# A prologue in another order: one tap row written and read back to front, w_in in halves on two queues, one staging pool, loads and casts spread over the fill

## The chip, the cores and the metric

The kernel runs on one core of a Trainium2 chip. The metric is the device time of one execution in microseconds (us); the runs before the change are three, and their median counts. Engines are named as the profile names them: PE is TensorE (PEld its weight loads), DVE is VectorE, ACT is ScalarE, POOL is GpSimd, SP is SyncE, which here only issues DMAs. ACT can issue DMAs too, on a queue of its own.

## The reference: what is computed

Two steps on x of 8 sequences, 4096 positions, 192 channels. First a causal convolution along the sequence with 7 taps, one set of taps for each of 8 heads of 24 channels, the taps being a softmax of `weight`. Then a two-layer network on every position:

```python
w = softmax(weight)                      # 8 heads x 7 taps
out[b, s, h] = sum_k w[h, k] * x_pad[b, s + k, h]
h = out.reshape(32768, 192) @ w_in       # 192 x 2048
g = h * cos(h)
return g @ w_out                         # 2048 x 192, float32
```

## The kernel before

**Layout.** The 8 sequences are 4 pairs (HB = 4): sequence b and sequence b + 4 go through together, each in one half (a lane) of 64 partitions. x is loaded in units: a unit is 4 blocks of 128 positions (112 new, 16 of overlap) of both sequences, two DMAs of 384 KB (`load_unit`, L83), staged as float32 (`xw`) and cast to bf16 (`xb`).

**The convolution** is a matrix product: for each head a 128x128 band matrix holds the 7 taps on diagonals, so a block of 128 positions times the band gives the 112 new ones. A work item is a pair of parts (a part is one unit and one of three channel groups of 64), 1024 columns in a PSUM tile `h` of two banks. The pool of `h` has three such tiles, for convolutions and for the network alike. In the normal form the product is split into two passes: `conv_first` (L249) uses the upper 64 partitions for one part and the lower 64 for the other, `conv_second` (L263) the other way round and adds. Between the passes a one-element memset on POOL (`changeover`, L199, tile `mark`) waits for the first pass and releases the second. `conv_out` (L266) copies the sum to bf16 (`ct`) on ACT or DVE and a DMA on SP transposes it to `cT`, channels by positions.

**The network** runs in steps of 128 of the 2048 hidden columns and 512 positions of both sequences: U (`up`, L293) makes `h` from `w1` (bf16 w_in) and `cT`; S (`sin`, L302) makes the cosine on ACT; M (`mult`, L307) makes g on DVE; 16 steps make a tile of positions. d (`down`, L314) multiplies g by `w2` (bf16 w_out) into two accumulators; x and y store them.

**The order** is written out by hand as a string of letters that `emit` (L349) reads; C, c and e are the two passes and the way out of a convolution. Each engine runs its instructions in that order. The prologue (L78 to L171, L375 to L386) loads and prepares everything; a fill follows (17 steps U, three convolutions, no d), and then one string is repeated until the end:

```python
emit("USM" * 2 + ("CUScMe" + "USM" * 3) * 3 + "USM" * 2 + "U")
while count["y"] < 2 * NI:
    emit("dddSMdUdMSdUdMSdUMdSUdSMdUdSMCdcdeMUdSdUyxUMS")
```

**The prologue's order.** On SP: wq (the taps' weights, sent to all 128 partitions, L79), six loads of units 0 and 1, eight pieces of w_in (L158: four chunks of 512 columns, each sent to both halves of the partitions), units 2 and 3, three transposes, four pieces of w_out (L168). On DVE and ACT the softmax is made on 128 partitions alike, seven products put the taps into `taps` (L132), and ACT writes all 128 rows to DRAM (L138) and reads them back shifted by one element a row, which makes the band (L139). POOL casts, in this order: halves of units 0 and 1, all of w_in, then the first marker, two parts of x, all of w_out, then the next marker. `prepare` (L238) casts the next pair and loads ahead after every second pass.

Of the kernel before, what the change touches and what calls it, by code (L numbers as in the profile page):

```python
# [16 lines left out]
def kernel(  # L17
# [29 lines left out]
    T = 512  # L47
# [16 lines left out]
    stage = ctx.enter_context(tc.tile_pool(name="stage", bufs=2))  # L64
    xw_pool = ctx.enter_context(tc.tile_pool(name="xw", bufs=3))
# [9 lines left out]
    ctx.enter_context(tc.manual_schedule())  # L75


    wq = consts.tile([128, H, K], FP32)  # L78
    nc.sync.dma_start(out=wq, in_=dram(weight, 0, [[0, 128], [1, H * K]]))  # L79

    xbs = {}

    def load_unit(b, u):  # L83

        xw = xw_pool.tile([128, 2, NB, D], FP32, name="xw")
        xb = xb_pool.tile([128, 2, NB, D], BF16, name="xb")
        if u == NU:
            rows = TAIL + 16
            nc.gpsimd.memset(xw[L:128, :, 0, :], 0.0)
            for s in range(2):  # L90
                base = ((s * HB + b) * S + UT * u - 16) * D
                nc.sync.dma_start(out=xw[0:rows, s, 0, :], in_=dram(x, base, [[D, rows], [1, D]]))
        elif u == 0:
            nc.gpsimd.memset(xw[0:16, :, 0, :], 0.0)
            for s in range(2):
                base = (s * HB + b) * S * D
                nc.sync.dma_start(out=xw[16:128, s, :, :], in_=dram(x, base, [[D, W], [W * D, NB], [1, D]]))
# [16 lines left out]


    ROW = H * 128 + 128
    taps = consts.tile([128, ROW], BF16)
    nc.gpsimd.memset(taps, 0.0)
    wmax = consts.tile([128, H], FP32)
    nc.vector.tensor_reduce(out=wmax, in_=wq, axis=AX.X, op=ALU.max)  # L120
    nc.vector.tensor_tensor(out=wq, in0=wq, in1=wmax.unsqueeze(2).to_broadcast([128, H, K]), op=ALU.subtract)  # L121
    wex = consts.tile([128, H, K], FP32)
    nc.scalar.activation(out=wex, in_=wq, func=AF.Exp)  # L123
    wsum = consts.tile([128, H], FP32)
    nc.vector.tensor_reduce(out=wsum, in_=wex, axis=AX.X, op=ALU.add)
    nc.vector.tensor_scalar(out=wsum, in0=wsum, scalar1=1e-9, scalar2=None, op0=ALU.add)
    winv = consts.tile([128, H], FP32)
    nc.vector.reciprocal(winv, wsum)
    tap = taps[:, 0:H * 128].rearrange("p (h j) -> p h j", h=H)
    for k in range(K):  # L130
        j = 127 - 10 - k
        nc.vector.tensor_tensor(out=tap[:, :, j:j + 1], in0=wex[:, :, k:k + 1], in1=winv.unsqueeze(2), op=ALU.mult)  # L132

    rows_d = d_pool.tile([128, ROW], BF16)
    band = consts.tile([128, H, 128], BF16)
    nc.scalar.dma_start(out=rows_d, in_=taps)  # L138
    nc.scalar.dma_start(out=band, in_=dram(rows_d, rows_d.offset + 127, [[ROW - 1, 128], [1, H * 128]]))  # L139
    warm = consts.tile([128, 1], FP32)  # L140
    nc.scalar.activation(out=warm, in_=winv[:, 0:1], func=AF.Sin, bias=0.0, scale=0.0)  # L141

    for u in range(2):
        load_unit(0, u)
        xw, xb = xbs[(0, u)]
        nc.gpsimd.tensor_copy(out=xb[:, 0, :, :], in_=xw[:, 0, :, :])
        nc.vector.tensor_copy(out=xb[:, 1, :, :], in_=xw[:, 1, :, :])  # L147


    w1 = consts.tile([128, NCH, Dff], BF16)  # L150
    w2 = consts.tile([128, NF, D], BF16)
    CW = Dff // 4

    def load_w1(c):
        cols = slice(c * CW, (c + 1) * CW)
        st = stage.tile([128, NCH, CW], FP32, name="st")
        for s in range(2):
            nc.sync.dma_start(out=st[s * L:(s + 1) * L], in_=dram(moe_w_in, c * CW, [[Dff, L], [L * Dff, NCH], [1, CW]]))  # L158
        if c == 0:
            nc.vector.tensor_copy(out=w1[:, 0:2, cols], in_=st[:, 0:2, :])  # L160
            nc.gpsimd.tensor_copy(out=w1[:, 2:, cols], in_=st[:, 2:, :])
        else:
            nc.gpsimd.tensor_copy(out=w1[:, :, cols], in_=st)  # L163

    def load_w2(c):
        n = NF // 4
        st = stage.tile([128, n, D], FP32, name="so")
        nc.sync.dma_start(out=st, in_=moe_w_out[c * CW:(c + 1) * CW, :].rearrange("(n p) d -> p n d", p=128))  # L168
        nc.gpsimd.tensor_copy(out=w2[:, c * n:(c + 1) * n, :], in_=st)  # L169

    load_w1(0)  # L171


    lane = (slice(0, L), slice(L, 128))
# [24 lines left out]
    def changeover(end):  # L199

        ins = nc.gpsimd.memset(mark, 0.0)  # L201
        order(ins, end)
        return ins
# [23 lines left out]
    pairs = []  # L227
    for b in range(HB):
        for u in range(1, NU, 2):
            pairs += [((b, u - 1, c), (b, u, c)) for c in range(NCH)]  # L230
# [7 lines left out]
    def prepare():  # L238

        c = state["cast"]  # L240
        if c < NC:
            for p in pairs[c]:
                cast_part(*p)
            state["cast"] += 1
        while state["loaded"] <= need[min(c + 2, NC - 1)]:
            load_unit(*units[state["loaded"]])
            state["loaded"] += 1

# [14 lines left out]
    def conv_second(mms, after):  # L263
        lanes(*mms, after=after)

    def conv_out(both, ps, copy=nc.scalar.copy):  # L266
# [14 lines left out]
        if u0 == u - 1 and u < NU:  # L281
            nc.sync.dma_start_transpose(out=dst(ch, u0, u + 1), in_=ct[0:W].rearrange("p k t -> p (k t)"))  # L282
        else:
            nc.sync.dma_start_transpose(out=dst(c0, u0, u0 + 1), in_=ct[0:W, 0, :])
# [64 lines left out]
    def emit(ops):  # L349
# [3 lines left out]
        for op in ops:  # L353
# [4 lines left out]
            elif op == "c":  # L358
                if "open" in state:
                    conv_second(state["open"][2], state.pop("mark"))  # L360
                    prepare()
            elif op == "e":
                if "open" in state:
                    conv_out(*state.pop("open")[:2])
# [7 lines left out]
                else:  # L372
                    {"U": up, "S": sin, "M": mult, "d": down}[op](n)

    for c in range(1, 4):  # L375
        load_w1(c)
    for u in (2, 3):
        load_unit(0, u)
    opened = [conv_first() for _ in range(3)]
    relay = changeover(opened[2][3])  # L380
    prepare()
# [39 lines left out]
```

## Time and profile before

| | before |
|---|---|
| runs | 759.79, 759.84, 759.93 us; median 759.84 |
| profiled execution | 760.31 us, span of its instructions 758.5 |
| PE busy | 709.8 us, 94% |
| DVE, ACT, POOL busy | 645.2, 589.8, 85.7 us |
| DMA | 73.49 MB, mean 97 GB/s |

All times in the profile count from the first instruction of the span. The timeline gives for each row its start, its length, the engine (a q behind it is the engine's issue of a DMA), the line, the operation with the tile it writes and those it reads, the shapes and the count; in brackets is the idle time of the engine before it, and what ended that. The windows view gives busy times by stretch. The DMA issues give size and median time from issue to landing.

### The profile page before, as it was taken

How to read it: one execution, taken by the hardware profiler on the slowest of the kernel's cores; microseconds unless marked ns; L12 is line 12 of the kernel's file. 1: busy time of each engine (PE TensorE's matmuls, PEld its weight loads, DVE VectorE, ACT ScalarE, POOL GpSimd, SP SyncE). 2: the span in 40 equal slices, each digit the busy share in tenths (PEclk: the TensorE clock that was granted, in tenths of full speed). 3: DMA queues.
4: the chain of work that ended last, by engine and by line, in shares of the span. 5: the costliest groups of instructions: out<-in, count | busy, mean ns of one | idle time of the engine just before them, and what ended most of it. 6: DMA issues, size and time to landing. Idle time of an engine off the chain costs nothing.

```text
span 758.5 us, 26895 instructions
## 1 busy us (share of the span) xinstructions
PE 709.8 (94%) x12064; PEld 518.3 (68%) x12064; DVE 645.2 (85%) x592; ACT 589.8 (78%) x639; POOL 85.7 (11%) x247
## 2 busy tenths in 40 slices
PE   0358999999999999999999999999999999999997
PEld 0125777777777777777777777777777777777776
DVE  1058999989898998899898999989899999999992
ACT  1157888888888888888888888888888878788781
POOL 2221011101101110110111011101101100000000
PEclk9999999999999999999999999999999999999999
DMA  8952543426163644242715435426173221111112
GB/s 209 227 148 61 109 110 82 110 73 143 59 168 87 125 90 106 77 116 71 185 37 149 114 78 105 110 76 143 50 179 75 44 56 44 45 43 34 33 44 64
DMA packets 128099, 73.49 MB, mean 97 GB/s; under 512 B 54000, under 2 KB 126192, under 8 KB 127984
## 3 DMA queue, kind: packets, MB, share of 16 engines
q1 hardware_dynamic: 127696, 71.22, 38.4%
q8 instruction: 94, 1.54, 0.9%
q10 hardware_dynamic: 288, 0.56, 0.3%
q14 instruction: 21, 0.17, 0.1%
HBM read 33.71 MB, written 25.46 MB: 78 GB/s over the span
## 4 chain that ended last, share of the span: by engine, by line
PE 91%; DMA 4%; DVE 2%; ACT 1%; issue 1%; POOL 1%; SPq 1%; POOLq 0%; ACTq 0%
PE h L191 46%; PE acc L191 44%; DMA st<-in_moe_w_in_dram 2%; DVE g L309 2%; DMA so<-in_moe_w_out_dram 1%; DMA xw<-in_x_dram 1%; ACT cos L304 1%; SPq L282 0%; POOL w L163 0%; POOL w L169 0%; ACT ct L274 0%; SPq L158 0%; ACT osb L343 0%; DVE osb L343 0%; SPq L98 0%
## 5 line engine op out<-in xcount | busy, mean ns | idle before, releaser
L309 DVE TENSOR_TENSOR g<-h,cos 128x1024 bf16<-128x1024 f32 x512 | 609.9, 1221 | 45.7 <-ACT cos L304 33.8
L304 ACT ACTIVATE cos<-h 128x1024 bf16<-128x1024 f32 x512 | 515.0, 1025 | 113.2 <-PE h L191 95.3
L191 PE MATMUL acc<-w,g 64*128 64x192 bf16 x8192 | 428.1, 243 | 1.3 <-ACT osb L343 0.8
L191 PEld LDWEIGHTS <-g 64*128 64x128 bf16 x8192 | 353.2, 94 | 101.8 <-issue 1.2
L191 PE MATMUL h<-cT,w 64*128 64x512 bf16 x3072 | 410.8, 379 | 10.3 <-DMA cT<-ct 5.0
L191 PEld LDWEIGHTS <-w 64*128 64x128 bf16 x3072 | 148.7, 94 | 89.3 <-issue 16.8
L201 POOL MEMSET mark<- 1x1 f32 x118 | 10.5, 89 | 632.5 <-PE acc L191 453.6
L191 PE MATMUL h<-xb,band 64*128 64x192 bf16 (+4 forms) x800 | 45.3, 230 | 32.9 <-DMA band<-rows_d 19.4
L274 ACT CAST ct<-h 112x1024 bf16<-112x1024 f32 x51 | 51.6, 1013 | 25.8 <-PE h L191 20.6
L343 DVE COPY osb<-acc 128x384 f32<-128x384 f32 x64 | 35.7, 558 | 38.4 <-PE acc L191 38.3
L113 POOL CAST xb<-xw 128x512 bf16<-128x512 f32 x102 | 60.1, 618 | 3.5 <-DMA xw<-in_x_dram 2.6
L191 PEld LDWEIGHTS <-band 64*128 64x128 bf16 x800 | 28.1, 97 | 44.8 <-POOL mark L201 22.4
L343 ACT COPY osb<-acc 128x384 f32<-128x384 f32 x64 | 30.4, 475 | 11.1 <-PE acc L191 11.1
L274 DVE CAST ct<-h 112x1024 bf16<-112x1024 f32 x1 | 1.2, 1224 | 13.7 <-PE h L191 13.7
L141 ACT ACT_TABLE_LOAD x1 | 1.3, 1283 | 10.0 <-DVE w L160 10.0
L163 POOL CAST w<-st 128x1536 bf16<-128x1536 f32 x3 | 4.4, 1469 | 7.6 <-DMA st<-in_moe_w_in_dram 7.6
L169 POOL CAST w<-so 128x768 bf16<-128x768 f32 x4 | 3.3, 824 | 10.5 <-DMA so<-in_moe_w_out_dram 10.5
L120 DVE TENSOR_REDUCE wmax<-wq 128x8 f32<-128x56 f32 x1 | 0.2, 210 | 4.8 <-DMA wq<-in_weight_dram 4.8
L147 DVE CAST xb<-xw 128x768 bf16<-128x768 f32 x2 | 1.1, 560 | 3.6 <-DMA xw<-in_x_dram 3.6
L160 DVE CAST w<-st 128x1024 bf16<-128x1024 f32 x1 | 0.7, 694 | 3.0 <-DMA st<-in_moe_w_in_dram 3.0
L271 ACT CAST ct<-h 112x512 bf16<-112x512 f32 x4 | 2.3, 587 | 0.9 <-PE h L191 0.9
L123 ACT ACTIVATE wex<-wq 128x56 f32<-128x56 f32 x1 | 0.3, 251 | 3.3 <-DVE wq L121 3.3
(18 smaller groups left out, 14.6 us busy)
## 6 DMA issues: line engine op xcount, KB each, us to landing
xw<-in_x_dram SPq DMA_DIRECT2D x64, 384.0 KB, 4.6
out_dram<-osb SPq DMA_DIRECT2D x64, 384.0 KB, 3.4
st<-in_moe_w_in_dram SPq DMA_DIRECT2D x8, 384.0 KB, 7.2
xw<-in_x_dram SPq DMA_DIRECT2D x8, 336.0 KB, 4.7
so<-in_moe_w_out_dram SPq DMA_DIRECT2D x4, 384.0 KB, 4.5
cT<-ct SPq DMA_TRANSPOSE x64, 3.4
xw<-in_x_dram SPq DMA_DIRECT2D x8, 60.0 KB, 1.9
xw<-in_x_dram SPq DMA_DIRECT2D x8, 36.0 KB, 3.9
```

The lines of the kernel that those rows point to most:

```text
L113: nc.gpsimd.tensor_copy(out=xb[:, :, :, ch], in_=xw[:, :, :, ch])
L141: nc.scalar.activation(out=warm, in_=winv[:, 0:1], func=AF.Sin, bias=0.0, scale=0.0)
L147: nc.vector.tensor_copy(out=xb[:, 1, :, :], in_=xw[:, 1, :, :])
L163: nc.gpsimd.tensor_copy(out=w1[:, :, cols], in_=st)
L169: nc.gpsimd.tensor_copy(out=w2[:, c * n:(c + 1) * n, :], in_=st)
L191: ins = nc.tensor.matmul(out=o, lhsT=w, rhs=r, start=start, stop=stop, skip_group_check=True)
L201: ins = nc.gpsimd.memset(mark, 0.0)
L271: nc.scalar.copy(ct[0:W, 0, :], ps[0:W, 0, :])
L274: copy(out=ct[0:W], in_=ps[0:W])
L304: nc.scalar.activation(out=cos, in_=hs[n], func=AF.Sin, bias=math.pi / 2.0, scale=1.0)
L309: nc.vector.tensor_tensor(out=g, in0=hs.pop(n), in1=cs.pop(n), op=ALU.mult)
L343: copy(out=osbs[k][:, 2 * bank:2 * bank + 2, :].rearrange("p a d -> p (a d)"), in_=acc[bank][:, 0:2 * D])
```

## The change

- The softmax is made on one partition. wq is loaded by ACT's queue instead of SP's; one product makes all taps. One row of 2.3 KB is written to DRAM by SP, behind the loads of x, and read back by SP to 128 partitions, each starting one element later (`turned`). The band is then `turned` with its columns read backwards, one half copied by DVE, the other by ACT.
- The casts of units 0 and 1 go to POOL and ACT instead of POOL and DVE.
- Of w_in each chunk's upper half goes on SP's queue and the lower on ACT's. It is cast in thirds (`cast_w1`), w_out is loaded in two pieces instead of four and cast in quarters of them (`cast_w2`). w_in and w_out use the same staging pool as x, now six buffers instead of three; the separate pool `stage` is gone.
- The first three pairs are convolved with all 128 partitions at once, without passes and marker. For units 2 and 3 the pairs are put together so that the first needs unit 2 alone.
- Loads and casts that stood ahead of the fill, or in `prepare`, are jobs in a generator; a letter k in the fill's string takes the next. `prepare` is split into `cast_pair` and `load_ahead`, called together by the letter p in the steady string.

The core of the diff (renamed and moved code that the text above tells is left out):

```diff
-    nc.sync.dma_start(out=wq, in_=dram(weight, 0, [[0, 128], [1, H * K]]))
+    nc.scalar.dma_start(out=wq, in_=dram(weight, 0, [[0, 1], [1, H * K]]))
...
-    for k in range(K):
-        j = 127 - 10 - k
-        nc.vector.tensor_tensor(out=tap[:, :, j:j + 1], in0=wex[:, :, k:k + 1], in1=winv.unsqueeze(2), op=ALU.mult)
+    nc.vector.tensor_tensor(out=tap[:, :, 9:9 + K], in0=wex, in1=winv.unsqueeze(2).to_broadcast([1, H, K]), op=ALU.mult)
...
-    nc.scalar.dma_start(out=rows_d, in_=taps)
-    nc.scalar.dma_start(out=band, in_=dram(rows_d, rows_d.offset + 127, [[ROW - 1, 128], [1, H * 128]]))
+    nc.sync.dma_start(out=row_d, in_=taps)
+    nc.sync.dma_start(out=turned, in_=dram(row_d, row_d.offset, [[1, 128], [1, H * 128]]))
+    for (u, s), copy in (((0, 0), nc.gpsimd.tensor_copy), ((0, 1), nc.scalar.copy),
+                         ((1, 0), nc.gpsimd.tensor_copy), ((1, 1), nc.scalar.copy)):
+        xw, xb = xbs[(0, u)]
+        copy(out=xb[:, s, :, :], in_=xw[:, s, :, :])
...
+    nc.vector.tensor_copy(out=band[:, 0:H // 2, :], in_=flip(turned[:, 0:H // 2, :]))
+    nc.scalar.copy(band[:, H // 2:H, :], flip(turned[:, H // 2:H, :]))
...
+        st = staged[1, c] = staging([NCH, CW])
+        for s, queue in enumerate((nc.sync, nc.scalar)):
+            queue.dma_start(out=st[s * L:(s + 1) * L], in_=dram(moe_w_in, c * CW, [[Dff, L], [L * Dff, NCH], [1, CW]]))
...
+            if (b, u) == (0, 3):
+                single = [(b, v, c) for v in (u - 1, u) for c in range(NCH)]
+                pairs += list(zip(single[::2], single[1::2]))
...
-    opened = [conv_first() for _ in range(3)]
-    relay = changeover(opened[2][3])
-    prepare()
-    for k, o in enumerate(opened):
-        conv_second(o[2], relay)
-        conv_out(*o[:2], nc.vector.tensor_copy if k == 1 else nc.scalar.copy)
-    for c in range(4):
-        load_w2(c)
-
-    emit("USM" * 2 + ("CUScMe" + "USM" * 3) * 3 + "USM" * 2 + "U")
+    for c in range(3):
+        ps = h_pool.tile([128, 2, T], FP32, name="h")
+        for k, p in enumerate(pairs[c]):
+            for o, h, r, _ in part_mms(p, ps[:, k, :]):
+                nc.tensor.matmul(out=o, lhsT=band[:, h, :], rhs=r, start=True, stop=True)
+        conv_out(pairs[c], ps, nc.vector.tensor_copy if c == 1 else nc.scalar.copy)
+    state["conv"] = 3
+    cast_w1(0, 0, nc.vector.tensor_copy)
+    cast_w1(0, 1)
+    cast_w1(0, 2, nc.vector.tensor_copy)
...
+    def later():
+        yield from (lambda q=q: cast_w1(1, q) for q in range(NCH))
+        yield lambda: load_unit(0, 2)
+        yield lambda: load_w1(2)
+        yield lambda: [load_unit(0, 3), load_w1(3), load_w2(0), load_w2(1)]
+        yield cast_pair
+        yield from (lambda q=q: cast_w1(2, q) for q in range(NCH))
+        yield cast_pair
+        yield load_ahead
+        yield from (lambda q=q: cast_w1(3, q) for q in range(NCH))
+        yield cast_pair
+        yield from (lambda c=c, q=q: cast_w2(c, q) for c in range(2) for q in range(4))
+        yield cast_pair
...
+    fill("kkkkUkSkMUSMUSMkUSMUSMCUScMekkkUSMkkUSMUSMCUScMekkkUSMkUSMkkkkUSMCUScMekkkkUSMUSMkU")
     while count["y"] < 2 * NI:
-        emit("dddSMdUdMSdUdMSdUMdSUdSMdUdSMCdcdeMUdSdUyxUMS")
+        emit("dddSMdUdMSdUdMSdUMdSUdSMdUdSMCdcpdeMUdSdUyxUMS")
```

How the order changes on POOL and on ACT, from the casts of units 0 and 1 into the fill. POOL before the change (st and so are the staged w_in and w_out, w_134 and w_135 their bf16 copies, mark the markers):

```order
L146 CAST xb<-xw 128x768 x2
L161 CAST w_134<-st 128x512
L163 CAST w_134<-st 128x3x512 x3
L201 MEMSET mark 1x1
L113 CAST xb<-xw 128x8x64 x2
L169 CAST w_135<-so 128x768 x4
L201 MEMSET mark 1x1
```

POOL after the change (everything is staged in xw; w_128 is w_in, w_129 w_out):

```order
L152 CAST xb<-xw 128x768 x2
L175 CAST w_128<-xw 128x512 x4
L119 CAST xb<-xw 128x8x64 x2
L218 MEMSET mark 1x1
L175 CAST w_128<-xw 128x512 x3
L119 CAST xb<-xw 128x8x64 x2
L218 MEMSET mark 1x1
L175 CAST w_128<-xw 128x512 x3
L119 CAST xb<-xw 128x8x64 x2
L185 CAST w_129<-xw 128x384 x4
L218 MEMSET mark 1x1
```

The first marker had all four chunks of w_in ahead of it and the second all of w_out; now the first one that is left has a third of chunk 0 and chunk 1 ahead of it, the second chunk 2, and the third chunk 3 and the first half of w_out.

ACT before the change, from the exponential of the softmax to the first cosines (rows_d is the DRAM copy of the tap rows):

```order
L123 ACTIVATE wex<-wq 128x56
L138 DMA rows_d<-taps 128x1152
L139 DMA band<-rows_d 128x1024
L141 ACT_TABLE_LOAD
L141 ACTIVATE warm<-winv 128x1
L274 CAST ct<-h 112x1024 x2
L304 ACTIVATE cos<-h 128x1024 x3
```

ACT after the change (the DMAs of in_moe_w_in are the lower halves of w_in's chunks):

```order
L131 ACTIVATE wex<-wq 1x56
L133 ACT_TABLE_LOAD
L133 ACTIVATE warm<-wex 1x1
L152 CAST xb<-xw 128x768 x2
L160 COPY band<-turned 128x512
L172 DMA xw<-in_moe_w_in_dram 64x3x512 x2
L297 CAST ct<-h 112x1024 x2
L172 DMA xw<-in_moe_w_in_dram 64x3x512
L327 ACTIVATE cos<-h 128x1024
L172 DMA xw<-in_moe_w_in_dram 64x3x512
```

The two DMAs of the taps went to SP; two casts of x and half the flip came, and four DMAs of w_in, two of them between the flip and the first ct.

More of the change, by code (lines that the diff above doesn't have):

```diff
@@ L116 @@
     ROW = H * 128 + 128
-    taps = consts.tile([128, ROW], BF16)
+    taps = consts.tile([1, ROW], BF16)
     nc.gpsimd.memset(taps, 0.0)
-    wmax = consts.tile([128, H], FP32)
+    for u in range(2):
+        load_unit(0, u)
+    wmax = consts.tile([1, H], FP32)
     nc.vector.tensor_reduce(out=wmax, in_=wq, axis=AX.X, op=ALU.max)
-    nc.vector.tensor_tensor(out=wq, in0=wq, in1=wmax.unsqueeze(2).to_broadcast([128, H, K]), op=ALU.subtract)
-    wex = consts.tile([128, H, K], FP32)
+    nc.vector.tensor_tensor(out=wq, in0=wq, in1=wmax.unsqueeze(2).to_broadcast([1, H, K]), op=ALU.subtract)
@@ L140 @@
[L140 to L144, printed above, removed]
-        xw, xb = xbs[(0, u)]
-        nc.gpsimd.tensor_copy(out=xb[:, 0, :, :], in_=xw[:, 0, :, :])
-        nc.vector.tensor_copy(out=xb[:, 1, :, :], in_=xw[:, 1, :, :])
+    tap = taps[:, 128:ROW].rearrange("p (h j) -> p h j", h=H)
+    nc.vector.tensor_tensor(out=tap[:, :, 9:9 + K], in0=wex, in1=winv.unsqueeze(2).to_broadcast([1, H, K]), op=ALU.mult)
@@ L171 @@
     load_w1(0)
+    load_w1(1)
     lane = (slice(0, L), slice(L, 128))
@@ L236, with cast_pair, load_ahead @@
     state = {"conv": 0, "loaded": 4, "cast": 3}
[L238 to L242, printed above, removed]
+    def cast_pair():
+        if state["cast"] < NC:
+            for p in pairs[state["cast"]]:
                 cast_part(*p)
             state["cast"] += 1
-        while state["loaded"] <= need[min(c + 2, NC - 1)]:
+    def load_ahead():
+        while state["loaded"] <= need[min(state["cast"] + 1, NC - 1)]:
             load_unit(*units[state["loaded"]])
@@ L360, in emit @@
                     conv_second(state["open"][2], state.pop("mark"))
-                    prepare()
+            elif op == "p":
+                cast_pair()
+                load_ahead()
             elif op == "e":
```

68 lines of the change are left out of this document (39 added, 29 removed).

## The prediction

> **What bounds the kernel now.** I read the page first, then the windows by stage, then the timeline and the waits of the first 66 us.
>
> The page's slices (a slice is 19 us) show TensorE nearly idle in the first two, half used in the third, and full after that:
>
> ```profile
> span 758.5 us, 26895 instructions
> PE   0358999999999999999999999999999999999997
> ```
>
> The windows view, cut at the first w_out product (65.54) and at the start of the fill (36.44). Columns: stretch, its length, busy time of PE, PEld, DVE, ACT, POOL, the granted clock, the DMA share, GB/s.
>
> ```profile
> 11.50:14.50 3.00, 0.00 (x0) 0.00 (x0) 0.30 (x1) 0.00 (x0) 0.00 (x0) 1.00 1.06 291
> 18.50:20.50 2.00, 1.08 (x18) 1.04 (x20) 0.00 (x0) 0.00 (x0) 1.47 (x1) 1.00 1.04 229
> 26.00:30.00 4.00, 1.46 (x20) 1.04 (x20) 0.82 (x1) 1.25 (x2) 2.11 (x3) 1.00 1.11 326
> 31.00:35.50 4.50, 1.22 (x4) 0.24 (x5) 0.00 (x0) 0.00 (x0) 0.61 (x1) 1.00 0.89 161
> 36.44:65.54 29.10, 17.48 (x136) 7.42 (x134) 17.47 (x15) 18.66 (x19) 6.92 (x13) 1.00 0.54 146
> 65.54:754.40 688.86, 687.51 (x11884) 508.21 (x11880) 622.43 (x561) 565.71 (x614) 68.61 (x219) 1.00 0.36 89
> ```
>
> From 65.54 to 754.40 TensorE works 687.51 of 688.86 us. The steady loop's text is unchanged apart from a `prepare` split into `cast_pair` and `load_ahead` called together, so I move this block as a whole: **the new time is the old one minus what the first w_out product gains on 65.54.** Everything is decided ahead of it, and there the timeline shows these steps:
>
> ```profile
> 0.75 0.41 SPq L79 DMA_DIRECT2D wq<-in_weight_dram  x1
> 1.21 0.42 SPq L97 DMA_DIRECT2D xw<-in_x_dram  x1
> 4.85 0.21 DVE L120 TENSOR_REDUCE wmax<-wq 128x8 f32<-128x56 f32 x1 [4.85 <-DMA wq<-in_weight_dram]
> 6.39 0.66 DVE L132 TENSOR_TENSOR taps<-wex,winv 128x8 bf16<-128x8 f32 x7
> 9.12 0.83 POOL L146 CAST xb<-xw 128x768 bf16<-128x768 f32 x1 [1.41 <-DMA xw<-in_x_dram]
> 15.25 0.33 ACTq L139 DMA_DIRECT2D band<-rows_d  x1
> 19.42 1.46 PE L191 MATMUL h<-xb,band 64*128 64x192 bf16 x20 [19.42 <-DMA band<-rows_d]
> 26.55 1.47 POOL L163 CAST w<-st 128x1536 bf16<-128x1536 f32 x1 [1.99 <-DMA st<-in_moe_w_in_dram]
> 28.10 1.46 PE L191 MATMUL h<-xb,band 64*128 64x192 bf16 x20 [7.22 <-POOL mark L201]
> 28.75 1.93 ACT L274 CAST ct<-h 112x1024 bf16<-112x1024 f32 x2 [11.65 <-PE h L191]
> 29.79 4.04 SPq L282 DMA_TRANSPOSE cT<-ct  x3
> 33.27 0.61 PE L191 MATMUL h<-cT,w 64*128 64x512 bf16 x2 [3.71 <-DMA cT<-ct]
> 35.79 1.89 PE L191 MATMUL h<-cT,w 64*128 64x512 bf16 x8 [0.47 <-DMA cT<-ct]
> 36.44 1.02 ACT L304 ACTIVATE cos<-h 128x1024 bf16<-128x1024 f32 x1 [5.76 <-PE h L191]
> 45.80 0.61 PE L191 MATMUL h<-xb,band 64*128 64x192 bf16 x6 [5.56 <-POOL mark L201]
> 65.54 1.50 PE L191 MATMUL acc<-w,g 64*128 64x192 bf16 x32
> ```
>
> Four waits follow each other: the band (19.42), a marker on POOL that stands behind three w_in casts (28.10), the transposes (to 35.79), and a second marker behind the w_out casts (45.80, a stall of 5.56).
>
> **The change, part by part.** I date each step anew, to the first cosine (36.44 now) and then to the first w_out product.
>
> *Taps.* They end at 7.05 today because wq lands at 4.85. One row instead of 128, on ACT's queue at the start, lands between the 1.9 us of the shortest x load and the 4.1 of today:
>
> ```profile
> band<-rows_d ACTq DMA_DIRECT2D x1, 256.0 KB, 4.1
> rows_d<-taps ACTq DMA_DIRECT2D x1, 288.0 KB, 8.0
> wq<-in_weight_dram SPq DMA_DIRECT2D x1, 28.0 KB, 4.1
> xw<-in_x_dram SPq DMA_DIRECT2D x8, 60.0 KB, 1.9
> ```
>
> From 4.85 to 7.05 is 2.2 us; six of seven tap products go (0.5). So the row is ready at 4.5 to 6.5. That earns nothing: its write stands on SP's queue behind six x loads, which are in flight until about 10. Row by row: unit 1's first half is cast at 9.12, its second half, 384 KB, (393 kB) would need 393/326 = 1.2 us more without w_in behind it, so 10.3, and the loads start 0.46 earlier (0.75 for 1.21): 9.85. I let the one-row write land with them, at 10.0. Today's takes 8.0 us from issue because it is 288 KB among x and w_in.
>
> *Read back.* Same shape as today's band, which took 4.1 us beside w_in; nothing is ahead of it now, and 1.9 is the lower end. I take 3.2, nearer to the same shape: 13.3 with the issue. Only an upper end by bytes makes it dear (rival 5).
>
> *Flip.* Not in the trace: 128x512 on DVE and on ACT at once. Nearest is ACT's cast of 512 columns, 0.59; from 0.2 to 0.7. Band ready at 13.9, for 19.42.
>
> ```profile
> L271 ACT CAST ct<-h 112x512 bf16<-112x512 f32 x4 | 2.3, 587 | 0.9 <-PE h L191 0.9
> ```
>
> *Casts of x* on POOL and ACT (today POOL and DVE, 0.83 a piece) end near 10.7, covered by the wait for the read back; uncovered they would cost 0.8.
>
> *Convolution of the first three pairs.* Whole-height products instead of two lane passes: half as many instructions, the same columns. Twice 1.46 for three pairs is 0.97 per pair; pair 0 ends at 14.9. The marker between the passes is gone, and with it the 7.22 us wait. On POOL it stood behind all w_in casts, the next one behind all w_out casts; the first marker that is left has one chunk of w_in and a third ahead of it, no w_out, while w_out's first half now stands ahead of the third.
>
> *ACT's queue* gets DMA issues. ACT issues nothing of w_in before it has flipped its half of the band, and two issues stand between that and the first ct. One such issue costs 0.6 on SP today:
>
> ```profile
> L158 SPq DMA_DIRECT2D st<-in_moe_w_in_dram x8: 595/604/732, 4.8 to 20.8; - x8
> 30.50:31.00 0.50, 0.00 (x0) 0.00 (x0) 0.00 (x0) 0.18 (x1) 0.00 (x0) 1.00 0.05 14
> 31.00:31.50 0.50, 0.00 (x0) 0.00 (x0) 0.00 (x0) 0.00 (x0) 0.22 (x1) 1.00 0.75 136
> ```
>
> 13.9 + 1.2 = 15.1, then ct 1.02, and the first transpose is issued at 16.2. Today 29.79 to 35.79 is 6.0 us from that issue to the third piece's use: 22.2. Then 0.65 (35.79 to 36.44): first cosine at 22.8 if the DMA engines are free.
>
> *They are not.* Two w_in pieces are on SP's queue from 10.5, two on ACT's from 13.9, a third at 17.7: five times 393 kB, 1.97 MB. With two queues I take the 291 GB/s of 11.5 to 14.5, when two queues moved data: 6.8 us from 12.4, to 19.2. The transposes flow from 17.4 (today from 31.0, 1.2 us after their issue, by the two short windows) and use 0.89 of the DMA themselves, so 1.8 us of w_in must be shared less the 0.5 they leave free in 4.5: **1.3 us** (ends 0 and 3.1). First cosine: **24.1**, 12.3 earlier.
>
> The Trainium skill, "DMA: Bandwidth & Descriptors" (Rules for kernel authors), speaks against this edit: two transfers to disjoint partition halves serialize, and spreading them over queues brings no bandwidth. The trace half disagrees: 291 GB/s with two queues against 229 with one at the same share, though the second stream was a write to DRAM. By the rule the sum takes 229 (rival 1).
>
> *The fill.* From the first cosine to the first w_out product the chain holds 14 products g, since the 17th w_in tile takes the PSUM tile, one of three, that the 14th one leaves. The rows of the undisturbed part:
>
> ```profile
> 46.20 4.04 PE L191 MATMUL h<-cT,w 64*128 64x512 bf16 x18
> 52.63 0.82 PE L191 MATMUL h<-cT,w 64*128 64x512 bf16 x6
> 55.20 3.49 DVE L309 TENSOR_TENSOR g<-h,cos 128x1024 bf16<-128x1024 f32 x3 [0.60 <-ACT cos L304]
> 59.53 1.23 DVE L309 TENSOR_TENSOR g<-h,cos 128x1024 bf16<-128x1024 f32 x1 [0.84 <-ACT cos L304]
> 61.35 6.88 DVE L309 TENSOR_TENSOR g<-h,cos 128x1024 bf16<-128x1024 f32 x6 [0.60 <-ACT cos L304]
> 28.99 0.61 POOL L113 CAST xb<-xw 128x512 bf16<-128x512 f32 x1 [0.94 <-DMA xw<-in_x_dram]
> ```
>
> Four steps with a convolution take 61.35 − 55.20 = 6.15; a step without one 6.88/6 = 1.15. Cosine 1.02 + three such groups 18.45 + two steps 2.3 + the last tile 0.65 = 22.5. At first TensorE needs 4.04/3 = 1.35 a tile instead of 0.82, though the granted clock says 1.00; that exceeds a step's 1.15 by 0.2, and three such steps make 0.6. **23.1.** Today's 29.1 less the 5.56 stall is 23.5, the same within 0.4. First w_out product: 24.1 + 23.1 = **47.2**, gain **18.3**.
>
> *What is late next.* Behind the transposes (22.7) come 11 pieces of 393 kB. Unit 2's x is cast at 22.7 + 2.4 + 1 (landing) + 1.2 = 27.3, for a first convolution five tiles in, about 29.3. Unit 3's stands behind w_in: 1.97 MB at 326 to 229 GB/s, 1 us, five casts of 0.61, so 32.8 to 35.4, for the second at 29.3 + 6.15 = 35.5. w_out's first half (nine pieces, 3.54 MB, and 1.6 of casts) at 36.2 to 40.8 for the third marker at 41.6, its second half by 44.2 for 47.2. All are covered, the second one barely. More staging buffers change nothing in the steady loop, where TensorE is full already.
>
> The profiled execution took 760.31 (span 758.5, 1.8 around it), 0.47 above the median of 759.84: 742.0 against the profile, **741.5** against the median.
>
> **The rivals.**
> 1. *Two queues bring no rate.* At 229 GB/s the w_in pieces end 1.8 later, the transposes with them: 743.3. For it: the share is full either way. Chance 0.15.
> 2. *The fill starves.* If loads run 10% under 229, unit 3 is 1 us late at the second convolution and w_out's first casts hold the third marker up to 2.5: 745.0. For it: the slack of 0.2 at the slow end. Against: 326 in plain x loads. 0.13.
> 3. *No sharing, short read back.* Sharing 0, read back 2.6, no slow start: 741.5 − 1.3 − 0.6 − 0.6 = 739.0. 0.14.
> 4. *TensorE stays slow through the fill.* Each round of a PSUM tile then lasts 0.7 longer (1.35 for 0.65), and 17 tiles on three are six rounds: 4.2, of which 0.6 is counted: 745.1. Against: today it speeds up by 52.63. The Trainium skill, "TensorE: Matmul & The Clock Gate" (Part 1), lets the clock rise after about 3.4 us of sustained work; by that it would rise here too. 0.07.
> 5. *The other side: slower.* All 128 partitions read the same 2.3 KB of DRAM at 2-byte offsets, where today each has its row. If such reads queue at one place, wq's 28 KB in 4.1 us is the only like case; by bytes that is 256/28 × 4.1 = 37 us for the read back, 34 more: 775. It decides above 3.2 + 18.3 = 21.5 us. Against: wq's time was shared with the start of x. 0.03.
>
> **How the numbers follow.** Forecast 0.48; the likeliest is 741.5. Low 737: rival 3 with the first transposes another 2 earlier (row write not held by x). High 748: rivals 2 and 4 with 2.5 more of either; only rival 5 and tails lie outside. 0.2% (1.5 us) is about what a measurement can tell from no change. Faster 0.96, same 0.01, slower 0.03.
>
> **What would show it.** Right: first convolution product near 13.9 with whole height, no marker ahead of the first cosine at about 24, no PE wait over 3 us after it, first w_out product near 47, and about 689 us from there to the last. Wrong: a band after 20, a second or third convolution waiting for POOL, or a steady part over 690.

## The result and the profile after

| | before | after |
|---|---|---|
| median | 759.82 us (759.64 to 759.93) | 741.58 us (741.02 to 741.76) |
| ratio | | 0.9759, interval 0.9742 to 0.9776 |
| span of the profiled execution | 758.5 | 739.7 |
| first cosine | 36.44 | 24.24 |
| first w_out product | 65.54 | 46.70 |

The kernel is 18.2 us faster; the forecast was 18.3. In the spans the gain has two parts: the fill starts 12.2 us earlier (36.44 − 24.24), and it takes 22.46 instead of 29.10, 6.6 less. What follows is as long as before: 739.7 − 46.70 = 693.0, and 758.5 − 65.54 = 693.0.

The page of after, span and TensorE by slices of 18.5 us. By the digits of the first four slices TensorE is idle for 1.7 slices, where it was for 2.4 before:

```profile
span 739.7 us, 26852 instructions
PE   1589999999999999999999999999999999999997
```

The windows of after, with the same columns as those of before (the last four: POOL's busy time, granted clock, DMA share, GB/s; a share above 1 is read as full):

```profile
13.50:17.50 4.00, 1.23 (x10) 0.83 (x7) 1.22 (x1) 1.58 (x2) 0.00 (x0) 1.00 1.06 205
17.50:21.00 3.50, 0.00 (x0) 0.00 (x0) 1.18 (x2) 0.00 (x0) 2.38 (x4) 1.00 1.17 200
29.50:32.00 2.50, 1.69 (x22) 0.94 (x19) 1.84 (x2) 1.11 (x2) 2.40 (x6) 1.00 1.06 339
24.24:46.70 22.46, 15.30 (x137) 6.82 (x135) 16.98 (x15) 17.80 (x19) 11.91 (x25) 1.00 1.03 265
46.70:735.56 688.86, 687.55 (x11884) 508.45 (x11880) 622.88 (x561) 565.45 (x614) 68.33 (x219) 1.00 0.36 90
```

The last row is the steady block, with the same 11884 products and the same busy time as before. In the fill's row the DMA engines are full on average (1.03 and 265 GB/s, against 0.54 and 146 before): what was loaded ahead of the fill is now loaded within it. And the first two rows show the DMA engines full but carrying only 200 to 205 GB/s, where 339 are reached at the same share as in the first row (third row). From 13.5 to 17.5 nearly all of it is w_in, half a chunk at a time; from 17.5 to 21 it is mostly the third chunk's lower half and the first transposes.

The steps ahead of the fill and the first ones in it, from the timeline of after:

```profile
3.60 0.21 DVE L140 TENSOR_TENSOR taps<-wex,winv 1x56 bf16<-1x56 f32 x1
3.84 0.31 SPq L147 DMA_DIRECT2D row_d<-taps  x1
8.27 0.35 SPq L148 DMA_DIRECT2D turned<-row_d  x1
11.63 0.62 ACT L160 COPY band<-turned 128x512 bf16<-128x512 bf16 x1 [1.63 <-DMA turned<-row_d]
11.63 0.29 DVE L159 COPY band<-turned 128x512 bf16<-128x512 bf16 x1 [7.83 <-DMA turned<-row_d]
11.64 1.35 ACTq L172 DMA_DIRECT2D xw<-in_moe_w_in_dram  x2
11.99 2.74 PE L404 MATMUL h<-xb,band 128*128 128x192 bf16 x20 [11.99 <-DVE band L159]
13.06 1.01 ACT L297 CAST ct<-h 112x1024 bf16<-112x1024 f32 x1 [0.81 <-PE h L404]
14.10 5.54 SPq L305 DMA_TRANSPOSE cT<-ct  x3
14.77 0.60 ACTq L172 DMA_DIRECT2D xw<-in_moe_w_in_dram  x1
22.04 0.63 SPq L172 DMA_DIRECT2D xw<-in_moe_w_in_dram  x1
22.35 1.08 PE L208 MATMUL h<-cT,w 64*128 64x512 bf16 x4 [7.62 <-DMA cT<-ct]
23.59 4.09 PE L208 MATMUL h<-cT,w 64*128 64x512 bf16 x20 [0.17 <-DMA cT<-ct]
24.24 1.02 ACT L327 ACTIVATE cos<-h 128x1024 bf16<-128x1024 f32 x1 [8.46 <-PE h L208]
27.85 0.82 PE L208 MATMUL h<-cT,w 64*128 64x512 bf16 x6 [0.17 <-DVE g L332]
29.60 0.09 POOL L218 MEMSET mark<- 1x1 f32 x1 [2.23 <-PE h L208]
46.70 1.50 PE L208 MATMUL acc<-w,g 64*128 64x192 bf16 x32
```

The two waits for a marker of before (7.22 and 5.56 us) are gone. A marker is now something that POOL waits for (2.23 us idle ahead of the one at 29.60), not something that TensorE waits for. Two waits of over 1 us are left: 11.99 for the band and 7.62 for the transposes.

### The profile page after: what moved, and what is told of

Same layout as the page of the kernel before. It is cut to its first block, busy times and chain, and to the rows that moved or that the text cites. A ratio compares the mean times of both kernels' runs of the same rounds, so it can differ in the third digit from the quotient of the medians.

```text
span 739.7 us, 26852 instructions
## 1 busy us (share of the span) xinstructions
PE 707.4 (96%) x12044; PEld 518.1 (70%) x12044; DVE 644.3 (87%) x586; ACT 591.1 (80%) x642; POOL 86.1 (12%) x256
## 4 chain that ended last, share of the span: by engine, by line
PE 93%; DVE 2%; DMA 2%; ACT 1%; issue 1%; SPq 0%; ACTq 0%; POOLq 0%; POOL 0%; DVEq 0%
PE h L208 48%; PE acc L208 45%; DVE g L332 2%; DMA cT<-ct 1%; ACT cos L327 1%; DMA row_d<-taps 1%; DMA turned<-row_d 0%; SPq L305 0%; ACT ct L297 0%; ACT L131 0%; PE h L404 0%; ACT osb L366 0%; DVE osb L366 0%; ACTq L78 0%; DVE band L159 0%
## 5 line engine op out<-in xcount | busy, mean ns | idle before, releaser
L208 PEld LDWEIGHTS <-w 64*128 64x128 bf16 x3072 | 148.7, 94 | 91.1 <-issue 18.5
L208 PE MATMUL h<-xb,band 64*128 64x192 bf16 (+5 forms) x760 | 41.7, 223 | 1.9 <-DVE g L332 1.9
L208 PEld LDWEIGHTS <-band 64*128 64x128 bf16 x760 | 25.8, 94 | 12.3 <-POOL mark L218 8.3
L404 PE MATMUL h<-xb,band 128*128 128x192 bf16 (+2 forms) x20 | 2.7, 330 | 12.0 <-DVE band L159 12.0
L404 PEld LDWEIGHTS <-band 128*128 128x128 bf16 x20 | 2.3, 143 | 12.1 <-DVE band L159 12.0
L175 POOL CAST w<-xw 128x512 bf16<-128x512 f32 x10 | 6.1, 641 | 9.7 <-DMA xw<-in_moe_w_in_dram 9.7
L152 ACT CAST xb<-xw 128x768 bf16<-128x768 f32 x2 | 1.7, 831 | 4.0 <-DMA xw<-in_x_dram 4.0
L185 POOL CAST w<-xw 128x384 bf16<-128x384 f32 x8 | 3.7, 512 | 0.0
```

The lines of the kernel that those rows point to most:

```text
L152: copy(out=xb[:, s, :, :], in_=xw[:, s, :, :])
L175: copy(out=w1[:, q, c * CW:(c + 1) * CW], in_=staged[1, c][:, q, :])
L185: nc.gpsimd.tensor_copy(out=w2[:, c * n:(c + 1) * n, :][:, fs, :], in_=staged[2, c][:, fs, :])
L208: ins = nc.tensor.matmul(out=o, lhsT=w, rhs=r, start=start, stop=stop, skip_group_check=True)
L404: nc.tensor.matmul(out=o, lhsT=band[:, h, :], rhs=r, start=True, stop=True)
```

## The experiments

First cosine and first w_out product are read from each profile; the fill is what lies between. Each ran beside the kernel before; their times beside the medians of before on the same chip (759.8 to 760.5) move by less than 0.7.

| label | what differs | median, us | first cosine | first w_out product | fill |
|---|---|---|---|---|---|
| (after) | | 741.58 | 24.24 | 46.70 | 22.46 |
| e1_old_band | old band | 745.54 | 28.22 | 50.68 | 22.46 |
| e2_new_band_only | before with the new band | 760.39 | 37.27 | 65.71 | 28.44 |
| e5_wout_first | all w_out casts ahead of the first marker | 750.28 | 24.68 | 55.82 | 31.14 |
| e3_one_queue | both w_in halves on SP | 747.51 | 22.29 | 49.88 | 27.59 |
| e4_third_late | third lower half issued later | 743.79 | 22.41 | 49.35 | 26.94 |
| e6_pair_first_two | two chunks' halves issued together | 741.54 | 23.91 | 46.51 | 22.60 |
| e7_pair_three | three chunks' halves together | 742.11 | 23.99 | 46.31 | 22.32 |
| e8_one_wide_dma | one DMA over 128 partitions | 743.07 | 21.16 | 46.69 | 25.53 |
| e11_third_on_sp | third lower half on SP | 745.87 | 22.32 | 51.14 | 28.82 |
| e12_third_on_pool | third lower half on POOL's queue | 746.18 | 22.41 | 50.06 | 27.65 |

(e9 and e10 stand apart below.) The table holds the main finding: every variant whose fill starts at 22.41 or earlier pays 3.1 to 6.4 us more in the fill. The loss is not in the first tiles: the granted clock reads 0.50 there in e3, e8 and e12 and 1.00 in after, but from the first cosine to the first product of the fill's first convolution it is 4.9 us in all four (in after 24.24 to 29.14).

**What the band is worth: e1 and e2.** e1 puts the old band into the kernel after, e2 the new band, and nothing else, into the kernel before.

```diff
-    nc.sync.dma_start(out=row_d, in_=taps)
-    nc.sync.dma_start(out=turned, in_=dram(row_d, row_d.offset, [[1, 128], [1, H * 128]]))
+    nc.scalar.dma_start(out=rows_d, in_=taps)
+    nc.scalar.dma_start(out=band, in_=dram(rows_d, rows_d.offset + 127, [[ROW - 1, 128], [1, H * 128]]))
```

> The changed kernel with the band made as before: taps on 128 partitions, 288 KB of rows written and read back by ACT's queue, no flip; all the rest as changed. My theory (the band's date moves the first transposes, and those the fill): the band is ready near 17 instead of 12.0, the first transpose is issued near 19 instead of 14.1, but w_in is then out of its way, so the first cosine comes near 26.3 instead of 24.2: about 743.7 us. Rival (the transposes wait for w_in's traffic in any case, so the band's date is covered): 741 to 742.

> The kernel before with only the new band: one tap row, read back to front, flipped, and the casts of x as in the changed kernel. My theory: the second pass of the first three convolutions waits for the marker on POOL behind the w_in casts, which the band does not move (w_in starts some 3 us later behind the read back, and 0.5 MB of tap rows are no longer in its way), so 759 to 761 us. Rival (the band is what bound the start): 7 us less, about 753.

e1 took 745.54 us (ratio 0.9808, 0.9793 to 0.9823), 4.0 more than after: more than either theory had. e2 took 760.39 (1.0003, 0.9994 to 1.0012): no gain at all. The timeline of e1, then of e2:

```profile
15.63 0.33 ACTq L151 DMA_DIRECT2D band<-rows_d  x1
18.51 2.74 PE L395 MATMUL h<-xb,band 128*128 128x192 bf16 x20 [18.51 <-DMA band<-rows_d]
20.62 4.29 SPq L296 DMA_TRANSPOSE cT<-ct  x3
```

```profile
12.64 1.46 PE L198 MATMUL h<-xb,band 64*128 64x192 bf16 x20 [12.64 <-DVE band L153]
27.37 1.47 POOL L170 CAST w<-st 128x1536 bf16<-128x1536 f32 x1 [2.27 <-DMA st<-in_moe_w_in_dram]
28.78 0.09 POOL L208 MEMSET mark<- 1x1 f32 x1
28.92 1.46 PE L198 MATMUL h<-xb,band 64*128 64x192 bf16 x20 [14.82 <-POOL mark L208]
```

In e2 the band is there 6.8 us earlier than before (12.64 for 19.42), and TensorE then waits 14.82 for the marker behind the w_in casts instead of 7.22. The next wait in the row takes the whole gain. No run puts this marker back into the kernel after, so what its removal is worth there is read from these two waits and not measured by itself. In e1 the band comes 6.5 later than in after (18.51 for 11.99), but the first cosine only 4.0: from the transposes' issue to the cosine it is 7.6 there (28.22 − 20.62) and 10.1 in after, since by then more of the first two chunks has been loaded.

**The place of w_out's casts: e5.** All eight are put ahead of the first marker that is left, as they stood ahead of the second one before.

```diff
+        yield lambda: [cast_w2(c, q) for c in range(2) for q in range(4)]
...
-        yield from (lambda c=c, q=q: cast_w2(c, q) for c in range(2) for q in range(4))
```

> The changed kernel with one thing put back: on POOL all eight casts of w_out stand ahead of the fill's first convolution marker, as they did before the change. My theory (the marker's place on POOL is what the fill paid for): the first marker waits for w_out, which lands at 37.5 in the changed kernel, plus two casts of 0.45: it runs near 39.5 instead of 29.6, so about 9 to 10 us more, 751. Rival (the fill is bound by its loads anyway, and the order of POOL is a detail): under 744.

Measured: 750.28 us (0.9865, 0.985 to 0.988), 8.7 more than after. POOL's and TensorE's rows in the timeline of e5:

```profile
35.70 1.86 POOL L185 CAST w<-xw 128x384 bf16<-128x384 f32 x4 [7.89 <-DMA xw<-in_moe_w_out_dram]
39.85 0.09 POOL L218 MEMSET mark<- 1x1 f32 x1
39.99 0.61 PE L208 MATMUL h<-xb,band 64*128 64x64 bf16 x7 [8.32 <-POOL mark L218]
```

The wait is back in full, 8.32 us: a marker stands behind casts, and these behind a load. That the order on POOL is worth this much is shown by this run, at about what its theory said (751); nothing else differs but the letters that go with it.

**The second queue: e3.**

```diff
-        for s, queue in enumerate((nc.sync, nc.scalar)):
+        for s, queue in enumerate((nc.sync, nc.sync)):
```

> The changed kernel with both halves of every w_in chunk on SP's queue. My theory after the trace of the changed kernel: the ACT half only flowed once the SP half was done, near 200 GB/s, and the third chunk's ACT half stood ahead of the second transpose; on one queue the transposes come behind two chunks alone, so the first cosine comes near 22.5 instead of 24.2: about 740 us. Rival, the one of my prediction (two queues move 291 GB/s, one 229): w_in ends 1.9 us later and the transposes with it, about 743.5.

Measured: 747.51 us (0.9838, 0.9821 to 0.9854), 5.9 more than after, more than either theory had. And the loss is not at the start: the first cosine comes 1.95 *earlier* (22.29), since four halves of w_in instead of five are ahead of the transposes. Then the fill lacks data; the timeline of e3:

```profile
20.23 5.51 PE L208 MATMUL h<-cT,w 64*128 64x512 bf16 x24 [5.25 <-DMA cT<-ct]
35.59 0.58 PE L208 MATMUL h<-xb,band 64*128 64x192 bf16 x5 [2.02 <-POOL xb L119]
35.89 1.56 PE L208 MATMUL h<-cT,w 64*128 64x512 bf16 x6
49.50 0.61 PE L208 MATMUL h<-cT,w 64*128 64x512 bf16 x2 [2.63 <-DMA cT<-ct]
49.88 2.79 PE L208 MATMUL acc<-w,g 64*128 64x192 bf16 x32
```

It waits for unit 3 of x (2.02) and for the third convolution's transposes (2.63), and after each such wait the next products take about twice as long (six in 1.56 instead of 0.82, 32 in 2.79 instead of 1.50).

**Less ahead of the transposes: e4, e11, e12.** The third chunk's lower half stands on ACT's queue at 14.77 in after, while its upper half comes at 22.04 on SP's. e4 issues the lower one behind the first cosine (one k moves in the fill's string), e11 on SP right behind the upper one, e12 on POOL's queue at about the time of the upper one.

```diff
-    fill("kkkkUkSkMUSM...
+    fill("kkkkUSkkMUSM...
...
+        for s, queue in enumerate((nc.sync, nc.sync if c == 2 else nc.scalar)):
...
+        for s, queue in enumerate((nc.sync, nc.gpsimd if c == 2 else nc.scalar)):
```

> The changed kernel with one move: ACT issues its half of w_in's third chunk behind the first cosine instead of ahead of it. My theory (384 KB, needed only by the ninth tile, run through the DMA engines between the first and the second transpose): 1.8 us less, about 739.8. Rival (the transposes are slow by themselves when they are issued close together): 741.6, no change.

> As the changed kernel, but the third chunk's lower half goes on SP's queue right behind its upper half, so that only two halves stand ahead of the first transposes on ACT's queue. First w_in tile near 20.4 instead of 22.35, as when that half was issued late; the chunk should land by 28 to 30, ahead of the ninth tile near 31. If so 739.5 to 740.5. Rival (what is gained at the start is paid in the fill): TensorE waits over 1 us at the ninth tile or the second convolution, and the total is 741.5 or more.

> As the changed kernel, but the third chunk's lower half is issued by POOL, behind the casts of the second chunk, at about the time that SP issues the upper half, so that only two halves stand ahead of the first transposes on ACT's queue and the third chunk's halves still go side by side. If it is the rate of supply in the fill (side by side about 330 GB/s, one half alone about 200) that took back the earlier start of the variants before, the first w_in tile starts near 20.3, the loads run near 330 from 23 to 35, TensorE waits under 1 us behind the first tiles, the first w_out product comes at 44.5 to 45.5, and the total is 739 to 740.5. Rival (an earlier start is paid in the fill whatever the order of loads): a wait for loads over 1 us, total 741.5 or more.

Measured: 743.79 (0.9784, 0.9769 to 0.9799), 745.87 (0.9809, 0.9792 to 0.9826) and 746.18 (0.9832, 0.981 to 0.9853): each slower than after, with e11 and e12 in the range of their rivals and e4 outside both of its theories (e4's interval just touches that of after, but its four runs take 743.5 to 744.2 us, those of after 741.0 to 741.8). In all three the first cosine is 1.8 to 1.9 us earlier, as expected, so this half alone costs the transposes that much. Then TensorE waits: in e4 for w_in, in e11 and e12 for x of unit 3. One row of the timeline of each:

```profile
35.16 1.73 PE L208 MATMUL h<-cT,w 64*128 64x512 bf16 x6 [2.92 <-POOL w L175]
```

```profile
37.31 0.38 PE L208 MATMUL h<-xb,band 64*128 64x192 bf16 x5 [3.87 <-POOL xb L119]
```

```profile
37.48 0.58 PE L208 MATMUL h<-xb,band 64*128 64x192 bf16 x5 [3.79 <-POOL xb L119]
```

Why the loads are late is seen in the windows from 29 to 35, of after first, then of e11:

```profile
29.00:32.00 3.00, 2.05 (x26) 1.22 (x27) 2.34 (x3) 1.61 (x2) 2.40 (x6) 1.00 1.06 336
32.00:35.00 3.00, 1.69 (x15) 0.56 (x11) 2.22 (x2) 3.00 (x5) 0.52 (x1) 1.00 1.11 327
```

```profile
29.00:32.00 3.00, 2.03 (x24) 0.87 (x18) 1.56 (x3) 2.95 (x4) 1.48 (x3) 1.00 1.12 200
32.00:35.00 3.00, 0.90 (x7) 0.19 (x4) 3.00 (x3) 1.82 (x2) 0.81 (x2) 1.00 1.13 194
```

The DMA engines are full in both (1.06 to 1.13), but e11's carry 200 and 194 GB/s where after's carry 336 and 327. That is 0.8 MB less in these six us (6 × 134 GB/s), two pieces of w_in. From 23 to 29 e11 is already behind, with 223 and 201 GB/s against 328 and 250 in after, and there at shares of 0.93 and 0.98. Issuing the two halves at about the same time (e12: 193 GB/s from 32 to 35) did not bring the rate back.

**The halves side by side: e6, e7.** Both issue the lower halves as soon as the row of taps has landed, instead of behind the flip (and give one cast of x to DVE); e6 for two chunks, e7 for three.

```diff
+    gate = row_w
...
+            if s == 1 and gate is not None:
+                order(ins, gate)
```

> The changed kernel with ACT's halves of w_in's first two chunks issued ahead of the flip, right when the row write has landed, so next to SP's halves (the last cast of x goes to DVE for that). My theory after the first runs (DMAs of both queues are served in the order of issue; a half alone writes 64 partitions at about 200 GB/s, both halves in flight together run near 330): the two chunks are in by about 15 instead of 18.3, the transposes come earlier, first cosine near 22 instead of 24.2: 739 to 740. Rival (16 engines are the limit, pairing brings nothing): 741 to 742.

> As the run that pairs the first two chunks, with the third chunk paired too, ahead of the transposes on both queues. My theory: 1.2 us of w_in more ahead of the transposes at 330 GB/s, but none between them, and 384 KB at 200 GB/s less in the fill: 739 to 740.5, no starving in the fill. Rival (any w_in ahead of the transposes costs its full time): 743.

Measured: 741.54 (0.975, 0.9736 to 0.9765) and 742.11 (0.9757, 0.9742 to 0.9771): both the same as after, e6 in the range of its rival, e7 between its two theories. The windows of e6, then of e7, while w_in flows:

```profile
13.50:16.00 2.50, 1.49 (x13) 1.08 (x10) 1.51 (x2) 1.80 (x2) 0.26 (x1) 1.00 1.06 214
```

```profile
13.50:16.00 2.50, 1.49 (x12) 1.07 (x10) 1.53 (x2) 1.80 (x2) 0.28 (x1) 1.00 1.07 220
16.00:19.50 3.50, 0.00 (x0) 0.00 (x0) 0.87 (x2) 0.04 (x1) 0.91 (x2) 1.00 1.05 313
```

Up to 16 the halves still took turns in both (214 and 220 GB/s), although they were issued together (at 8.51 and 8.11 in e6). From 16 to 19.5, in e7, the packets of both queues flowed side by side, and 313 GB/s were reached at the same share. But e7 also has a sixth half ahead of the transposes, so its first cosine is only 0.25 earlier than after's.

**Partitions or queues: e8, e9, e10.** e8 fills all 128 partitions with one DMA on SP's queue; it reads other rows of w_in than the reference needs (bytes, shape and count are the same), so that part of the computation is changed. e9 loads the right rows to both halves by a source that begins with two copies, and e10 is e9 with w_out's second half behind the first convolution's transposes.

```diff
+        nc.sync.dma_start(out=st, in_=dram(moe_w_in, c * CW, [[Dff, 128], [32 * Dff, NCH], [1, CW]]))
...
+        for q in range(NCH):
+            nc.sync.dma_start(out=st[:, q, :], in_=dram(moe_w_in, q * L * Dff + c * CW, [[0, 2], [Dff, L], [1, CW]]))
...
-        yield lambda: [load_unit(0, 3), load_w1(3), load_w2(0), load_w2(1)]
+        yield lambda: [load_unit(0, 3), load_w1(3), load_w2(0)]
...
-        yield load_ahead
+        yield lambda: load_w2(1)
```

> The changed kernel with each w_in chunk loaded by one DMA on SP's queue that writes all 128 partitions; as many bytes in as many runs of 2 KB, but other rows of w_in, so the output is not the reference's. It tells the number of queues from the number of partitions. If partitions are what counts (a half writes 64): packets of 2 KB near 100 ns as with two halves in flight, first cosine near 22, about 739. If it takes two queues: packets near 170 ns, the fill starves as with both halves on SP, about 747.

> Each chunk of w_in is loaded by three DMAs on SP's queue, each over all 128 partitions (the same rows to both halves), none on ACT's queue; all of it is computed as in the reference. If the number of partitions sets the rate, these loads run as the wide ones did, the first w_in tile starts near 20.5, and the total is that of the wide DMA or somewhat better: 740 to 743, since the fill still waits for loads and the third convolution's transposes. Rival (it takes two queues): as with both halves on one queue, 746 to 748.

> As the wide thirds, but w_out's second half is issued behind the first convolution's transposes, and the loads ahead behind the second's, so that the transposes do not stand behind 1.5 MB of w_out. If it is the order of supply in the fill that takes back the earlier start, no wait of TensorE over 1 us is left after the first w_in tiles, the first w_out product comes 22.5 after a first cosine near 21.5 to 22, so at 44 to 45, and the total is 738 to 739.5. Rival (the DMA engines' total rate bounds the fill, whatever the order): within 1 us of the wide thirds.

e8: 743.07 us (0.9759, 0.9737 to 0.9782), between its two theories and the same as after. Its windows and its timeline:

```profile
13.50:17.50 4.00, 1.41 (x12) 1.01 (x10) 2.40 (x3) 1.77 (x2) 0.87 (x1) 1.00 1.10 279
29.00:32.00 3.00, 1.95 (x16) 0.53 (x11) 2.14 (x2) 3.00 (x4) 2.16 (x4) 1.00 1.07 358
```

```profile
20.52 5.46 PE L207 MATMUL h<-cT,w 64*128 64x512 bf16 x26 [0.48 <-DMA cT<-ct]
30.77 4.56 SPq L306 DMA_TRANSPOSE cT<-ct  x1
46.31 0.61 PE L207 MATMUL h<-cT,w 64*128 64x512 bf16 x2 [2.57 <-DMA cT<-ct]
46.69 2.79 PE L207 MATMUL acc<-w,g 64*128 64x192 bf16 x32
```

One queue carries 279 where after, with two, carried 205 in the same window: so it doesn't take two queues; together with e7 this fits a rate that is set by how many partitions are being filled. e8's DMA is also twice as large, 768 KB; but the loads of x, 384 KB each over 128 partitions, ran at 326 GB/s in before (26 to 30), so the size is not what it takes. The earliest first cosine of all (21.16) is spent at the end of the fill: the issue of the first convolution's transpose, which stands behind w_out's loads on SP's queue, takes 4.56 us, all that SP issues later is late (the third convolution's result is ready at 42.44 and its transpose is issued at 43.51), and TensorE waits 2.57 for the third convolution's transposes and then runs slow products.

e9 took 792.78 (1.0424, 1.041 to 1.0438), far outside both theories, e10 787.87 (1.0361, 1.0347 to 1.0375), outside both of its own. The windows of e9:

```profile
17.50:21.00 3.50, 0.00 (x0) 0.00 (x0) 0.00 (x0) 0.00 (x0) 0.00 (x0) 1.00 0.13 49
```

A share of 0.13 is 2 of 16 DMA engines, and 49 GB/s take 5.3 us for each 256 KB piece. So e9 says nothing about partitions. What e10 changes against e9 is still readable: 4.9 us less, and the wait for the last transposes (3.42 in e9) is gone. It is the order on SP's queue that made them late.

## Why the prediction was right, point by point

The total was right to 0.1 us and so was its frame: the steady block moved unchanged, the gain was the first w_out product's (18.8 by the spans, forecast 18.3), and it came from the start and the vanished stall. That a piece of it can hide behind the next wait is shown by e2 (0), and that the order on POOL is a piece of its own by e5 (8.7 lost). That the total agrees to 0.1 us is luck: the first transpose came 2.1 us early, the contention behind it took 2.2 us too long, and the fill was 0.6 shorter; what is left, 0.5, is what the profiled run of before lay above the median.

- **Band**: forecast 13.9, measured 11.98. The taps were ready at 3.81 (forecast 4.5 to 6.5) and the row landed by 8.27, not with the end of x, which itself came by 9.17 instead of 10.0. The read back took 3.36 from its issue (8.27 to 11.63; forecast 3.2), the flip 0.29 and 0.62 (0.59).
- **ACT's two DMA issues**, charged at 1.2 in place of the convolution of 0.97 beside them: they cost nothing. ACT's queue issues them (11.64) while ACT copies its half of the band (11.63), and the ct at 13.06 waits for TensorE, not for them. With the band 1.9 earlier, and the 0.2 by which the issues had stood above the convolution gone, the first transpose went out at 14.10 instead of 16.2, 2.1 early.
- **Contention**, forecast 1.3 with ends 0 and 3.1: this is the term that failed. From the first transpose's issue to the first cosine the kernel took 10.14 us, before 6.65 (36.44 − 29.79): 3.5 us, above the upper end too. I took 291 GB/s because two queues were at work; they carried 200 to 205. Of the 3.5, the third chunk's lower half makes 1.9 to 2.1: with it gone, e4, e11 and e12 need 8.05 to 8.23 (transposes issued at 14.36, 14.09 and 14.26). With one wide DMA for each chunk (e8, issued at 14.28) it is 6.88, close to before. The third chunk's upper half was issued 7.3 us later (22.04), so the lower one stood there early for nothing; but moving it cost more in the fill than it gave.
- **Fill**: 22.46, forecast 23.1 and 22.5 without the slow start. The slow tiles were there (20 products in 4.09), but the first cosines came 1.28 apart, and the 0.13 a step over the 1.15 did not show at the end.
- **Late next**: x of unit 2 cast by 27.37 (forecast 27.3), of unit 3 by 32.53 (32.8 to 35.4), w_out's first half from 38.70 without a wait for data, for the third marker at 41.97 (forecast 41.6). In after unit 3 was 2.8 us early for the second convolution at 35.29; "the second one barely" was still the right warning: unit 3 is what e3, e11 and e12 wait for.
- **Readings**: in the first slices of before TensorE is busy 0, 3, 5 and 8 tenths, so the second is not nearly idle and the fourth not full; and DVE's casts of x took 0.56 there, not 0.83. Neither enters the sum.

The rivals: *no rate from two queues* was nearer to the rate at the start than the forecast, and wrong on what follows. There, two queues carried 200 to 205 GB/s, and yet without the second one (e3) the kernel loses 5.9, in the fill. *The fill starves* did not happen in after, but did in e3, e4, e11 and e12. *No sharing* fails with the 3.5 us of contention. *TensorE stays slow* fails at 27.85 (six products in 0.82). *Same-row reads queue up* fails with the read back's 3.36.

What stays open: when two halves run side by side, and when that gives the rate. By the packets of the two queues two halves of a chunk ran side by side in after from 30 to 32 (331 GB/s), in e6 from 29 to 32 (345) and in e7 from 16 to 19.5 (313); in e6 and e7 before 16 they took turns. And side by side was not enough elsewhere: in e7 from 29 to 32 the two queues had about half of the share each and moved 244 GB/s together, in e12 from 24 to 28 POOL's queue and SP's moved 197:

```profile
29.00:32.00 3.00, 2.02 (x25) 0.96 (x20) 2.16 (x3) 1.75 (x3) 2.78 (x6) 1.00 1.06 244
```

I have no rule that covers these. So it is shown that the rate in the fill differs at a full share, and that TensorE's waits there are for the loads that this delays; that the number of partitions sets the rate fits e8 and most stretches, but is not shown beyond these. That a better order could have both the early start and the rate was tried in three ways (e8, e11, e12) and not reached. No variant beats the kernel after.

## What to carry to other kernels

Date a chain of waits to its end before crediting a part: the same new band was worth 0 in the old order and 4.0 in the new one. A load ahead of a critical transfer costs time there (2 us for one half chunk), but moving it behind pays only if the stage that follows has supply to spare. So look at GB/s, not at the DMA share alone: 200 and 335 GB/s both read as full.

## What the runs showed of the hardware

- Loads that fill 64 partitions ran at 200 to 205 GB/s one at a time at a full share (after, 13.5 to 21, at the end with transposes), at 313 to 345 with the other half in flight (after, e6, e7), but once also at 244 (e7, 29 to 32), and one DMA over 128 partitions at 279 to 358 in windows with other work (e8). The Trainium skill, "DMA: Bandwidth & Descriptors" (Rules for kernel authors), says that two transfers to disjoint partition halves serialize and recommends one over 128 partitions. e8 agrees with the advice; that they serialize holds up to 16 us in e6 and e7 (214 and 220) and not behind that in e7 (313), and there the measurement decides.
- A source whose slowest dimension has two entries ran at a share of 0.13, as much as 2 of 16 DMA engines, and 49 GB/s. The Trainium skill, "DMA: Bandwidth & Descriptors" (Rules for kernel authors), says that a leading broadcast of c copies confines a DMA to at most c engines; e9 agrees.
- SP's issue of a transpose can take long behind loads on SP's queue, and all that stands behind it moves with it: 1.22 us in after's fill, 4.56 in e8, 7.4 to 8.5 in e3, e4, e11 and e12. It does not take 16 busy engines: in e9 three such issues behind six loads of w_in took 14.51 us, with a share of 0.13 from 29 to 33 and from 37 to 41, and ended at 43.84, just after the last of these loads had landed (its cast starts at 43.47).

```profile
29.33 14.51 SPq L305 DMA_TRANSPOSE cT<-ct  x3
```

- Waits of TensorE of 2 to 3 us within the fill were enough to slow the products behind them to about half speed (e3, e4, e8), at a granted clock of 0.50 in the windows of e4. The granted clock does not show every such stretch: after's first tiles were nearly as slow (20 products in 4.09 us, later six in 0.82) at a granted clock of 1.00. The row of e4 (columns: PE's busy time, granted clock, DMA share, GB/s):

```profile
35.00:37.00 2.00, 1.84 (x7) 0.50 1.11 226
```
